# Loading and transposing the gate weights of a mixture-of-experts kernel: one word-wise DMA against GpSimd rows and six PE transposes

## The chip, the cores and the metric

The kernel runs on one core of one Trainium2 chip. The metric is device time in microseconds for one execution, input tensors in DRAM to output in DRAM. The profile names the engines PE (TensorE matmuls), PEld (its weight loads), DVE (VectorE), ACT (ScalarE), POOL (GpSimd) and SP (SyncE, which issues nearly all DMAs here).

## The reference, cut to what matters

Three stages follow one another: an attention with a sigmoid in place of the softmax, a layer that takes the maximum of three projections, and a mixture of 8 experts. The change touches one input of the third, the gate weights `w_gate` (768 x 8 float32, 24 KB), which choose one expert for each token.

```python
scores = scale * np.matmul(q, k.transpose(0, 1, 3, 2)) - np.log(S)      # 4 x 12 heads, S = 448, D = 64
x = 1 / (1 + np.exp(-scores)) @ v                                      # -> 1792 tokens x 768
h = np.maximum(np.maximum(x @ w1, x @ w2), x @ w3)
x = h @ w_out
logits = x @ w_gate + modality_bias[modality_id]                       # w_gate: 768 x 8
e_idx = np.argmax(logits, axis=1)                                      # one expert of 8 for each token
...
out[mask] = gate_w[mask, None] * (np.maximum(x[mask] @ w1[e], 0) @ w2[e])
```

## The kernel before

The attention stage works on 24 units of two heads each, in 12 pairs (the loop over `j`, L379). For a unit, `split_qk` (L267, on DVE) splits the loaded q and k into a rounded part and a rest in `kq`; `emit_qk` (L287, on PE) makes the scores in three groups of six matmuls, each group followed by a sigmoid on ACT (L285); `emit_av` (L315, on PE) multiplies with v; `emit_qk_last` (L303) and `emit_av_last` (L323) do the last 64 of the 448 columns for both units of a pair; `evac_X` (L331, on DVE) brings the result into SBUF. The order on PE, ACT, DVE and SP is the order in which the code is written, and each engine runs its instructions in that order; GpSimd's come in the order of the code too. SP runs two pairs ahead: in pair j, behind `emit_qk_last(j)`, it issues the loads of q, k and v for the units of pair j + 2 (L254 to L265), and from the second pair on, in most second pairs, one chunk of the projection weights of the second stage (`stage`, L216), which DVE converts from 64-bit words a little at a time (`background`, L236).

`wgT` is a DRAM scratch tensor that holds the gate weights turned, as 8 rows of 768. Its only readers are eight DMAs in the second stage (L436), each of which spreads one row over all partitions; DVE then folds the gate weights into `w_out` (L439). The first of these is issued at 236.6 us of the span. In the fifth pair (j = 4) SP issues, ahead of that pair's weight chunk, four small transfers: `slots` (L400), `wgT` (L402), the modality bias `mb` (L403) and the modality numbers `midi` (L404). The transfer at L402 reads `w_gate` word by word so that it lands turned; `midi` is read in words of 8 bytes, 1792 of them; `mb` is 128 copies of 64 bytes.

At the start PE runs seven matmuls on constants (`warm`, L356) while the first loads are on their way, and GpSimd fills constants, the identity matrix `ident` among them. The tile `v4` (tag K1) holds the v of two units of six; in the second stage the same space holds the gate rows. PSUM tags: the scores go round `a0`, `a1` and `t`; `x0` and `x1` hold the results of the units, and `x1` the warm-up before them.

Of the kernel before, what the change touches and what calls it, by code (L numbers as in the profile page):

```python
# [28 lines left out]
def attn_moe_kernel(  # L29
# [15 lines left out]
    nc = tc.nc  # L45
    B, HP, D, _, _, S = qk.shape
    NT, DM = out.shape
    E, _, FF = ew1.shape
    KB = DM // 128
# [25 lines left out]
    def hold(tag, name, *shape):  # L75
        return pool.tile([128, *shape], F32, tag=tag, name=name)

    def r(ap):
        return ap.bitcast(F32R)

    def cut(a, off, *shape):

        n = 1
        for s in shape:
            n *= s
        a = a[:, off:off + n]
        if len(shape) == 2:
            a = a.rearrange("p (a b) -> p a b", a=shape[0])
        elif len(shape) == 3:
            a = a.rearrange("p (a b c) -> p a b c", a=shape[0], b=shape[1])  # L90
        return a
# [10 lines left out]
    NW = 2 * NJ  # L102
# [5 lines left out]
    kq = [cut(kq_, 4 * S * i, 2, 2, S) for i in range(2)]  # L108
    u1, u2, u3 = (hold(f"U{i}", f"u{i}", 2048) for i in range(3))
    qk_in = [cut(u, 2 * S * i, 2, S) for u in (u1, u2) for i in range(2)]  # L110
    v4 = hold("K1", "v4", 2, NW + 1, D)
    v_in = [cut(u3, (NW + 1) * D * i, NW + 1, D) for i in range(4)] + [v4[:, i] for i in range(2)]

    stage = [hold(f"S{i}", f"stage{i}", KB * 256).bitcast(I32) for i in range(2)]
# [7 lines left out]
    wgT = dram.tile([E, DM], F32, name="wgT")  # L122
# [3 lines left out]
    ident = cpool.tile([128, 128], F32, name="ident")  # L126
# [21 lines left out]
    def ps(tag, shape, name):  # L148
        return psum.tile(shape, F32, tag=tag, name=name)
# [60 lines left out]
    def load_chunk():  # L210
        i = loaded[0]
        if i < len(chunks):
            kind, a, b = chunks[i]
            loaded[0] += 1
            src, n = chunk_src(a, b) if kind == "w" else (woi[a * 128:(a + 1) * 128, :].rearrange("p (a c) -> p a c", a=1), 1)
            nc.sync.dma_start(out=stage[i % 2].rearrange("p (a c) -> p a c", a=n), in_=src)  # L216
# [19 lines left out]
    def background(us, stop=None, late=2):  # L236

        while us > 0 and (bg or bg2):
            if stop is not None and stop in ready:
                return  # L240
            if bg and (bg[0][2] is None or step[0] >= used.get(bg[0][2], 1e9) + late):
                op, cost, _ = bg.popleft()
            elif bg2 and loaded[0] > LAST_O and step[0] >= bg2[0][2]:
                op, cost, _ = bg2.popleft()
            else:
                return
            op()
            us -= cost


    def load_qk(u):
        b, hp = divmod(u, HP)
        for h in range(2):
            nc.sync.dma_start(out=qk_in[u % 4][D * h:D * (h + 1)], in_=qk[b, hp, :, h])  # L254

    def load_v(u):
        b, hp = divmod(u, HP)
        vt = v_in[u % 6]
        if u % 2 == 0:
            nc.sync.dma_start(out=vt, in_=v[b, hp])  # L260
            return

        nc.sync.dma_start(out=vt[:, 0:NW], in_=v[b, hp, :, 0:NW])
        for h in range(2):
            nc.sync.dma_start(out=vt[SR * (1 - h):SR * (2 - h), NW], in_=v[b, hp, SR * h:SR * (h + 1), NW])  # L265

    def split_qk(u):  # L267
        src, kt = qk_in[u % 4], kq[u % 2]
        if u == 0:
            nc.vector.tensor_copy(out=r(kt[:, 0, 0]), in_=src[:, 0])  # L270
            nc.scalar.activation(out=r(kt[:, 0, 1]), in_=src[:, 1], func=ACTF.Copy)
            for i in range(2):
                nc.vector.tensor_tensor(out=r(kt[:, 1, i]), in0=src[:, i], in1=kt[:, 0, i], op=ALU.subtract)
        else:
            nc.vector.tensor_copy(out=r(kt[:, 0]), in_=src)  # L275
            nc.vector.tensor_tensor(out=r(kt[:, 1]), in0=src, in1=kt[:, 0], op=ALU.subtract)
# [3 lines left out]
    def scores():  # L280
        s_n[0] += 1
        return ps(("a0", "a1", "t")[s_n[0] % 3], [128, 2, 512], "s")

    def sigmoid(dst, s):
        nc.scalar.activation(out=dst, in_=s[:, :, 0:S], func=ACTF.Sigmoid, scale=qscale, bias=nlns)  # L285

    def emit_qk(u):  # L287

        kt = kq[u % 2]
        for g in range(NJ):  # L290
            s = scores()
            for n, (a, x) in enumerate(((0, 0), (0, 1), (1, 0))):
                for h in range(2):
                    p = slice(D * h, D * (h + 1))
                    nc.tensor.matmul(s[:, h, 0:S], r(kt[p, a, 0, 128 * g:128 * (g + 1)]), r(kt[p, x, 1]),  # L295
                                     start=(n == 0), stop=(n == 2))
            sigmoid(atb[u % 2][:, 2 * g:2 * g + 2], s)

    def quarter(i, h):

        return slice(SR * (h ^ i), SR * ((h ^ i) + 1))

    def emit_qk_last(j):  # L303

        s = scores()
        for i in range(2):
            src = qk_in[(2 * j + i) % 4]
            for h in range(2):
                p = slice(D * h, D * (h + 1))
                nc.tensor.matmul(s[quarter(i, h), i, 0:S], src[p, 0, 128 * NJ:], src[p, 1], start=True, stop=True)  # L310
        sigmoid(atl[j % 2], s)
# [3 lines left out]
    def emit_av(u):  # L315
        X_t[u] = ps(f"x{u % 2}", [128, 512], "X")
        vt, at = v_in[u % 6], atb[u % 2]
        for g in range(NJ):
            for h in range(2):
                nc.tensor.matmul(X_t[u][64 * h:64 * h + 64, 0:S], vt[:, 2 * g + h], at[:, 2 * g + h],  # L320
                                 start=(g == 0), stop=False)

    def emit_av_last(j):  # L323
        for i in range(2):
            u = 2 * j + i
            for h in range(2):
                p = quarter(i, h)
                nc.tensor.matmul(X_t[u][64 * h:64 * h + 64, 0:S], v_in[u % 6][p, NW], atl[j % 2][p, i],  # L328
                                 start=False, stop=True)

    def evac_X(u):  # L331
        b, hp = divmod(u, HP)
        src = X_t.pop(u)[:, 0:S]
        dR = xR[hp][:, b * S:(b + 1) * S]
        dL = xL[hp][:, b * S:(b + 1) * S]
        nc.vector.tensor_copy(out=r(dR), in_=src)
        nc.vector.tensor_tensor(out=r(dL), in0=src, in1=dR, op=ALU.subtract)

    with tc.manual_schedule(engines={mybir.EngineType.PE, mybir.EngineType.Activation, mybir.EngineType.DVE, SP}):
        load_qk(0)  # L340
        nc.vector.memset(gw, 0.0)
        nc.vector.memset(ones, 1.0)
        make_identity(nc, ident)
# [35 lines left out]
        for j in range(NU // 2 + 1):  # L379
            A, B, more = 2 * j, 2 * j + 1, j < NU // 2  # L380
            if more:
                emit_qk(A)
            if j:
                emit_av(B - 2)
                emit_av_last(j - 1)
                evac_X(A - 2)
                evac_X(B - 2)
            if not more:
                break
            emit_qk_last(j)  # L390
            for u in (A + 4, B + 4):
                if u < NU:
                    load_qk(u)
                    load_v(u)
            if A + 2 < NU:
                split_qk(A + 2)
            if j == 1:
                load_chunk()
            if j == 4:
                nc.sync.dma_start(out=slots.rearrange("(p c) o -> p (c o)", p=128), in_=idx)  # L400
                with nc.allow_non_contiguous_dma(reason="small"):
                    nc.sync.dma_start(out=wgT, in_=w_gate.rearrange("d e -> e d"))  # L402
                nc.sync.dma_start(out=mb, in_=m_bias.partition_broadcast(128))  # L403
                nc.sync.dma_start(out=midi, in_=mid.bitcast(I32).rearrange("(i p t) -> p i t", p=128, t=2))  # L404
            if j >= 2:
                background(2.5, stop=(1, 0))
            emit_qk(B)
            emit_av(A)
            if B + 2 < NU:
                split_qk(B + 2)  # L410
# [491 lines left out]
        for p, (i, n) in enumerate(todo[:NF * NCH]):  # L902
# [9 lines left out]
            else:  # L912
                f = n - 2 * KB
# [27 lines left out]
        d = xo[xo_n[0] % 3]  # L941
# [7 lines left out]
    with tc.For_i(NSTAT, nreg, 1) as iv:  # L949
        nc.sync.dma_start(out=idx2, in_=slots.rearrange("(p c) o -> p (c o)", p=128)[:, bass.ds(iv * 2, 2)])  # L950
        nc.sync.dma_start(out=e_dyn, in_=exd[0:1, bass.ds(iv, 1)])
        e = nc.values_load(e_dyn[0:1, 0:1], engines=(SP,), min_val=0, max_val=E - 1)
# [51 lines left out]
```

## Time and profile before

| what | us |
|---|---|
| median of 3 runs (807.14 to 807.71) | 807.19 |
| the profiled execution's own time | 807.75 |
| its span, first to last instruction | 806.0 |
| PE busy in the span | 760.3 (94%) |
| DVE, ACT, POOL busy | 448.5, 258.6, 65.2 |

The profile is of one execution, and all its times are microseconds from the start of its span unless they are marked ns; 1.75 us of the execution's time lie around the span. A row of an engine in order of time has the start, the length, the engine, the line of the kernel, the operation with what it writes and reads, and the count of instructions merged into the row; in brackets is the idle time of the engine ahead of it and what ended it. A row of SP's queue is the time in which SP was busy with issuing DMAs, not that of their transfer. The row of a stretch has the busy time and the count of instructions of each engine, the clock granted to PE (1.00 is 2.4 GHz, 0.50 is 1.2 GHz), the mean busy share of the 16 DMA engines, and the rate of the bytes moved.

### The profile page before, as it was taken

Reading aid. Unit: us, or ns where it says so; the run is one execution under the profiler, and the core shown is the slowest. Engines: PE = TensorE matmul, PEld = TensorE weight load, DVE = VectorE, ACT = ScalarE, POOL = GpSimd, SP = SyncE. Lnnn points to the kernel's source line nnn. Section 1 sums busy time; section 2 is a strip of 40 time slices with the busy share of each in tenths; the row PEclk is TensorE's granted clock in tenths of the full one; section 3 lists DMA queues with packets and bytes.
Section 4 is the critical chain, followed back from the end, with each engine's and each line's share of the span. In section 5 each row is a group of like instructions: output and inputs, shape, how many; then the busy total and the mean of one; then the engine's idle time right before and its main releaser. Section 6 shows DMA issues by size and latency. Waiting matters only on the chain.

```text
span 806.0 us, 11821 instructions
## 1 busy us (share of the span) xinstructions
PE 760.3 (94%) x4698; PEld 642.0 (80%) x4698; DVE 448.5 (56%) x751; ACT 258.6 (32%) x362; POOL 65.2 (8%) x82
## 2 busy tenths in 40 slices
PE   9998059999999999999999999999999999999994
PEld 5454034479999999999997888998999999899993
DVE  3685047666696878784305822246665466555532
ACT  5665025520101010010003323245544445454522
POOL 0000000000000000000010060230220302021000
PEclk9999569999999999999999999999999999999998
DMA  8767596313242131220000196343657401064000
GB/s 206 206 148 2 3 225 164 109 40 118 77 153 83 59 117 59 79 79 1 0 1 1 54 368 243 102 144 133 249 171 263 157 22 59 14 246 148 20 25 18
DMA packets 50920, 88.04 MB, mean 109 GB/s; under 512 B 14219, under 2 KB 32908, under 8 KB 50862
## 3 DMA queue, kind: packets, MB, share of 16 engines
q1 hardware_dynamic: 47294, 75.71, 33.1%
q0 software_dynamic: 3568, 11.54, 4.3%
q8 instruction: 39, 0.64, 0.3%
q14 instruction: 19, 0.16, 0.1%
HBM read 94.95 MB, written 11.57 MB: 132 GB/s over the span
## 4 chain that ended last, share of the span: by engine, by line
PE 87%; SPq 6%; issue 2%; DMA 2%; DVE 1%; POOL 0%; ACT 0%; POOLq 0%; DVEq 0%
PE acc L457 33%; PE oacc L796 15%; PE hacc L775 14%; PE acc L523 7%; PE X L320 6%; PE s L295 5%; SPq L403 4%; PE acc2b L523 4%; DMA u<-in_qk_dram 2%; PE X L328 1%; PE xT L736 1%; PE s L310 1%; SPq L254 1%; PE lgp L483 1%; SPq L216 1%
## 5 line engine op out<-in xcount | busy, mean ns | idle before, releaser
L457 PE MATMUL acc<-xR,w_ring 128*128 128x448 f32 x864 | 210.5, 365 | 0.0
L457 PEld LDWEIGHTS acc<-xR,w_ring 128*128 128x128 f32 x864 | 162.2, 188 | 13.5 <-issue 0.7
L796 PE MATMUL oacc<-wo_ck,xh 128*128 128x512 f32 (+1 forms) x672 | 124.0, 340 | 0.0
L775 PE MATMUL hacc<-xh,wo_ck 128*128 128x256 f32 x1008 | 122.3, 283 | 0.0
L775 PEld LDWEIGHTS hacc<-xh,wo_ck 128*128 128x128 f32 x1008 | 121.9, 192 | 0.3
L796 PEld LDWEIGHTS oacc<-wo_ck,xh 128*128 128x128 f32 x672 | 102.8, 188 | 13.8
L285 ACT ACTIVATE at<-s,nlns 128x896 f32<-128x896 f32 x84 | 78.2, 1008 | 80.8 <-PE s L295 51.3
L457 PE MATMUL acc<-xLa,w_ring 128*128 128x448 f32 x360 | 102.2, 365 | 0.0
L295 PE MATMUL s<-kq 64*128 64x448 f32 x432 | 53.7, 388 | 31.8 <-DVE kq L275 31.2
L295 PEld LDWEIGHTS s<-kq 64*128 64x128 f32 x432 | 38.8, 190 | 54.2 <-issue 39.7
L182 DVE TENSOR_TENSOR wo_ck<-raw,wo_ck 128x512 fp32r<-128x512 f32 (+1 forms) x108 | 75.4, 743 | 6.0 <-ACT wo_ck L181 5.8
L523 PE MATMUL acc<-wo_ck,hs 128*128 128x512 f32 x252 | 77.4, 394 | 0.0
L457 PEld LDWEIGHTS acc<-xLa,w_ring 128*128 128x128 f32 x360 | 67.6, 188 | 5.3
L181 ACT ACTIVATE wo_ck<-raw 128x512 fp32r<-128x512 f32 (+1 forms) x108 | 67.0, 671 | 11.5 <-PE hacc L775 11.3
L523 PEld LDWEIGHTS acc<-wo_ck,hs 128*128 128x128 f32 x252 | 47.2, 188 | 11.4 <-ACT wo_ck L181 0.8
L523 PE MATMUL acc2b<-wo_ck,hs 128*128 128x256 f32 x252 | 56.2, 280 | 0.0
L439 DVE SCALAR_TENSOR_TENSOR gk<-wof,gk 128x768 f32<-128x768 f32 x48 | 45.9, 956 | 1.2
L461 ACT ACTIVATE hA<-acc 128x896 f32<-128x896 f32 x8 | 7.4, 920 | 115.1 <-PE acc L457 115.1
L782 DVE SCALAR_TENSOR_TENSOR xh<-hacc,xh 128x1024 fp32r<-128x1024 f32 x14 | 17.1, 1224 | 46.3 <-ACT xh L781 46.3
L727 POOL DMA_INDIRECT xg<-x2d,idx x30 | 30.0, 1000 | 148.2 <-PE xT L736 101.0
L523 PEld LDWEIGHTS acc2b<-wo_ck,hs 128*128 128x128 f32 x252 | 41.5, 189 | 0.1
L320 PE MATMUL X<-at,u 128*64 128x448 f32 x192 | 40.4, 557 | 0.0
(175 smaller groups left out, 666.5 us busy)
## 6 DMA issues: line engine op xcount, KB each, us to landing
raw<-in_moe_w_dram SPq DMA_DIRECT2D x24, 1024.0 KB
stage<-in_moe_w_dram SPq DMA_DIRECT2D x18, 768.0 KB
u<-in_qk_dram SPq DMA_DIRECT2D x48, 224.0 KB
raw<-in_moe_w_dram SPq DMA_DIRECT2D x12, 768.0 KB
raw_S<-in_moe_w_dram SPq DMA_DIRECT2D x12, 768.0 KB
stage<-in_moe_w_out_dram SPq DMA_DIRECT2D x6, 768.0 KB
x2d<-xo SPq DMA_DIRECT2D x14, 256.0 KB
gk<-wgT SPq DMA_DIRECT2D x8, 384.0 KB
```

Of the source, the lines that this page charges most:

```text
L181: nc.scalar.activation(out=r(dR), in_=src, func=ACTF.Copy)
L182: nc.vector.tensor_tensor(out=r(dL), in0=src, in1=dR, op=ALU.subtract)
L285: nc.scalar.activation(out=dst, in_=s[:, :, 0:S], func=ACTF.Sigmoid, scale=qscale, bias=nlns)
L295: nc.tensor.matmul(s[:, h, 0:S], r(kt[p, a, 0, 128 * g:128 * (g + 1)]), r(kt[p, x, 1]), start=(n == 0), stop=(n == 2))
L320: nc.tensor.matmul(X_t[u][64 * h:64 * h + 64, 0:S], vt[:, 2 * g + h], at[:, 2 * g + h], start=(g == 0), stop=False)
L403: nc.sync.dma_start(out=mb, in_=m_bias.partition_broadcast(128))
L439: nc.vector.scalar_tensor_tensor(out=junk, in0=wof[kb], scalar=1.0, in1=wgb[e % 2], op0=ALU.mult, op1=ALU.mult, accum_out=gw[:, kb, e:e + 1])
L457: nc.tensor.matmul(acc[:, c, 0:S], r(m[:, a, kk, :]), r(x[kk][:, c0 + S * c:c0 + S * (c + 1)]), start=(kk == 0 and n == 0), stop=(kk == KB ...
L523: nc.tensor.matmul(acc_t[t, c], r(hs[t][:, a, kk, :]), r(wo_rl[c][:, kk, b]), start=(kk == 0 and n == 0), stop=(kk == KB - 1 and n == 2))
L727: nc.gpsimd.indirect_dma_start(out=xg[i % 2][s][:, XC[c][0]:XC[c][1]], out_offset=None, in_=x2d[c], in_offset=bass.IndirectOffsetOnAxis(ap ...
L775: nc.tensor.matmul(acc[:, f], r(w[a][:, 128 * f:128 * (f + 1)]), r(x[:, kk]), start=(kk == 0 and m == 0 and f % 2 == 0), stop=(kk == KB - ...
L796: nc.tensor.matmul(dst, r(x[:, f, 128 * s:128 * (s + 1)]), r(w[a][:, c0:c1]), start=(f == 0 and m == 0 and not (shared and s == 1)), stop= ...
```

## The change

The word-wise DMA at L402 goes. In its place:

- GpSimd's queue, as its first instruction behind the program's start, loads `w_gate` in rows of 8 words (32 bytes; 128 partitions times 6 rows, 768 in all) into `wg_in`, a piece of the K1 tile that now is one tile of 2304 words a partition.
- In the first pair, behind `emit_qk_last(0)`, `turn_gate` puts six PE transposes (8 columns by 128 rows each) into PSUM tags `x0` and `x1`, and two DVE copies (8 x 512 and 8 x 256) into `wg_t`.
- GpSimd's queue writes `wg_t` to `wgT`, 8 rows of 3072 bytes, behind the constants.

```diff
--- before.py
+++ after.py
@@ -108,7 +108,10 @@
     kq = [cut(kq_, 4 * S * i, 2, 2, S) for i in range(2)]
     u1, u2, u3 = (hold(f"U{i}", f"u{i}", 2048) for i in range(3))
     qk_in = [cut(u, 2 * S * i, 2, S) for u in (u1, u2) for i in range(2)]
-    v4 = hold("K1", "v4", 2, NW + 1, D)
+    k1 = hold("K1", "k1", 3 * DM)
+    v4 = cut(k1, 0, 2, NW + 1, D)
+    wg_in = cut(k1, 2 * (NW + 1) * D, KB, E)
+    wg_t = k1[0:E, 2 * DM:3 * DM]
     v_in = [cut(u3, (NW + 1) * D * i, NW + 1, D) for i in range(4)] + [v4[:, i] for i in range(2)]
 
     stage = [hold(f"S{i}", f"stage{i}", KB * 256).bitcast(I32) for i in range(2)]
@@ -328,6 +331,15 @@
                 nc.tensor.matmul(X_t[u][64 * h:64 * h + 64, 0:S], v_in[u % 6][p, NW], atl[j % 2][p, i],
                                  start=False, stop=True)
 
+    def turn_gate():
+
+        for x, k0, k1 in ((0, 0, 4), (1, 4, KB)):
+            T = ps(f"x{x}", [128, 512], "wgp")
+            for k in range(k0, k1):
+                nc.tensor.transpose(T[0:E, 128 * (k - k0):128 * (k - k0 + 1)], wg_in[:, k], ident)
+            nc.vector.tensor_copy(out=wg_t[:, 128 * k0:128 * k1], in_=T[0:E, 0:128 * (k1 - k0)])
+        nc.gpsimd.dma_start(out=wgT, in_=wg_t)
+
     def evac_X(u):
         b, hp = divmod(u, HP)
         src = X_t.pop(u)[:, 0:S]
@@ -338,6 +350,7 @@
 
     with tc.manual_schedule(engines={mybir.EngineType.PE, mybir.EngineType.Activation, mybir.EngineType.DVE, SP}):
         load_qk(0)
+        nc.gpsimd.dma_start(out=wg_in, in_=w_gate.rearrange("(k p) e -> p k e", p=128))
         nc.vector.memset(gw, 0.0)
         nc.vector.memset(ones, 1.0)
         make_identity(nc, ident)
@@ -388,6 +401,8 @@
             if not more:
                 break
             emit_qk_last(j)
+            if not j:
+                turn_gate()
             for u in (A + 4, B + 4):
                 if u < NU:
                     load_qk(u)
@@ -398,8 +413,6 @@
                 load_chunk()
             if j == 4:
                 nc.sync.dma_start(out=slots.rearrange("(p c) o -> p (c o)", p=128), in_=idx)
-                with nc.allow_non_contiguous_dma(reason="small"):
-                    nc.sync.dma_start(out=wgT, in_=w_gate.rearrange("d e -> e d"))
                 nc.sync.dma_start(out=mb, in_=m_bias.partition_broadcast(128))
                 nc.sync.dma_start(out=midi, in_=mid.bitcast(I32).rearrange("(i p t) -> p i t", p=128, t=2))
             if j >= 2:
```

Lines of the kernel after are higher by 3 from L112 to L330, by 12 to L340, by 13 to L390, by 15 to L400 and by 13 from L403 on (numbers of the kernel before). In the rows below, `u` and `v` or `k` with a number are SBUF buffers, and the brackets name the semaphores waited for: DMASW that of a DMA from GpSimd's queue, DMAHW those of SP's, in turn eight of each, so that each DMA also waits for the one eight before it.

SP's queue, in the pair j = 4, before:

```order
L265 DMA u_73<-in_v_dram 64x64 [waits DMAHW1_49]
L400 DMA slots<-idx 128x30 [waits DMAHW2_49,Pool_49]
L402 DMA wgT<-in_moe_w_gate_dram 6144x1x1 [waits DMAHW3_49]
L403 DMA mb<-in_moe_modality_bias_dram 128x16 [waits DMAHW4_49]
L404 DMA midi<-in_moe_modality_id_dram 128x14x2 [waits DMAHW5_49]
L216 DMA stage_75<-in_moe_w_dram 128x6x256 [waits DMAHW6_49]
L254 DMA u_72<-in_qk_dram 64x896 [waits DMAHW7_49,DVE_49,PE_49]
```

and after:

```order
L268 DMA u_73<-in_v_dram 64x64 [waits DMAHW1_49]
L415 DMA slots<-idx 128x30 [waits DMAHW2_49,Pool_49]
L416 DMA mb<-in_moe_modality_bias_dram 128x16 [waits DMAHW3_49]
L417 DMA midi<-in_moe_modality_id_dram 128x14x2 [waits DMAHW4_49]
L219 DMA stage_75<-in_moe_w_dram 128x6x256 [waits DMAHW5_49]
L257 DMA u_72<-in_qk_dram 64x896 [waits DMAHW6_49,DVE_49,PE_49]
```

The four small transfers have become three; `mb`, `midi`, the chunk of weights and the next pair's loads follow `slots` in the same order, and each waits for the semaphore one number lower.

PE, in the first pair, before:

```order
L310 MATMUL s<-u_71 64x448 [waits DMAHW3_49]
L295 MATMUL s<-kq 128x448 [waits DVE_49,Activation_49]
L295 MATMUL s<-kq 128x448
L295 MATMUL s<-kq 128x448 [waits DVE_49]
L295 MATMUL s<-kq 128x448 x3
L295 MATMUL s<-kq 128x448 [waits Activation_49]
```

and after:

```order
L313 MATMUL s<-u_71 64x448 [waits DMAHW3_49]
L339 MATMUL wgp<-ident,k_74 8x128 [waits DMASW0_49,Pool_49]
L339 MATMUL wgp<-ident,k_74 8x128 x5
L298 MATMUL s<-kq 128x448 [waits DVE_49,Activation_49]
L298 MATMUL s<-kq 128x448
L298 MATMUL s<-kq 128x448 [waits DVE_49]
L298 MATMUL s<-kq 128x448 x3
L298 MATMUL s<-kq 128x448 [waits Activation_49]
```

The six transposes stand between `emit_qk_last(0)` and the scores of unit 1; the first waits for the rows of GpSimd's DMA and for the identity matrix.

DVE, in the first pair, before:

```order
L275 CAST kq<-u_71 128x896 [waits DMAHW3_49,DMAHW2_49]
L276 TENSOR_TENSOR kq<-u_71,kq 128x896 [waits DVE_49]
L275 CAST kq<-u_72 128x896 [waits DMAHW1_49,DMAHW0_49,PE_49]
L276 TENSOR_TENSOR kq<-u_72,kq 128x896 [waits DVE_49]
L275 CAST kq<-u_72 128x896 [waits DMAHW3_49,DMAHW2_49,PE_49]
```

and after:

```order
L278 CAST kq<-u_71 128x896 [waits DMAHW3_49,DMAHW2_49]
L279 TENSOR_TENSOR kq<-u_71,kq 128x896 [waits DVE_49]
L340 COPY k_74<-wgp 8x512 [waits PE_49]
L340 COPY k_74<-wgp 8x256 [waits PE_49]
L278 CAST kq<-u_72 128x896 [waits DMAHW1_49,DMAHW0_49]
L279 TENSOR_TENSOR kq<-u_72,kq 128x896 [waits DVE_49]
```

Two copies that wait for PE stand ahead of the split of unit 2.

## Rows read from the trace of the kernel before

**Rows 1.** The page's 40 slices of 20.15 us: PE's busy share in tenths

```profile
PE   9998059999999999999999999999999999999994
```

**Rows 2.** PE in order, 71.9 to 125: start us, us, instructions, idle before, releaser

```profile
72.72 0.93 PE L310 MATMUL s<-u 64*64 64x448 f32 x8
...
75.67 2.48 PE L320 MATMUL X<-at,u 128*64 128x448 f32 x12
109.37 0.74 PE L295 MATMUL s<-kq 64*128 64x448 f32 x2 [31.22 <-DVE kq L275]
...
117.73 0.93 PE L310 MATMUL s<-u 64*64 64x448 f32 x8
```

**Rows 3.** PE in order, 159 to 161: the last pair's rows of L310

```profile
160.04 0.93 PE L310 MATMUL s<-u 64*64 64x448 f32 x8
```

**Rows 4.** DVE in order, 74 to 110

```profile
74.78 0.62 DVE L337 TENSOR_TENSOR xLb<-X,xR 128x448 fp32r<-128x448 f32 x1
108.59 0.63 DVE L275 CAST kq<-u 128x896 fp32r<-128x896 f32 x1 [33.19 <-DMA u<-in_qk_dram]
```

**Rows 5.** SP's queue in order, 57 to 110: issues of DMAs

```profile
58.09 0.81 SPq L402 DMA_DIRECT2D wgT<-in_moe_w_gate_dram  x1
58.95 30.48 SPq L403 DMA_DIRECT2D mb<-n_moe_modality_bias_dram  x1
89.47 0.43 SPq L404 DMA_DIRECT2D midi<-in_moe_modality_id_dram  x1
89.95 4.43 SPq L216 DMA_DIRECT2D stage<-in_moe_w_dram  x1
```

**Rows 6.** Packets that the DMA engines moved from 61 to 90 us

```profile
DMA packets 5572, 0.04 MB, mean 1 GB/s; under 512 B 5571, under 2 KB 5571, under 8 KB 5571
```

**Rows 7.** Packets that the DMA engines moved from 91 to 99 us

```profile
DMA packets 1494, 0.02 MB, mean 3 GB/s; under 512 B 1491, under 2 KB 1494, under 8 KB 1494
```

**Rows 8.** Stretches: length, busy of five engines, granted clock, DMA share, GB/s

```profile
61.00:91.00 30.00, 17.14 (x126) 8.02 (x122) 11.01 (x16) 10.21 (x11) 0.00 (x0) 0.84 0.80 1
91.00:96.00 5.00, 0.00 (x0) 0.00 (x0) 0.00 (x0) 0.00 (x0) 0.00 (x0) 0.50 0.03 1
96.00:98.50 2.50, 0.00 (x0) 0.00 (x0) 0.00 (x0) 0.00 (x0) 0.00 (x0) 0.50 0.55 7
```

**Rows 9.** PE in order, 5.6 to 20.8: the first pair

```profile
6.12 0.49 PE L295 MATMUL s<-kq 64*128 64x448 f32 x2
...
9.63 2.63 PE L295 MATMUL s<-kq 64*128 64x448 f32 x18
12.20 2.48 PE L320 MATMUL X<-at,u 128*64 128x448 f32 x12
14.61 2.09 PE L295 MATMUL s<-kq 64*128 64x448 f32 x18
...
19.83 0.93 PE L310 MATMUL s<-u 64*64 64x448 f32 x8
```

**Rows 10.** DVE in order, 0 to 13

```profile
5.26 0.39 DVE L270 CAST kq<-u 128x448 fp32r<-128x448 f32 x1 [3.96 <-DMA u<-in_qk_dram]
...
10.64 0.63 DVE L275 CAST kq<-u 128x896 fp32r<-128x896 f32 x1 [1.68 <-PE s L295]
11.30 1.09 DVE L276 TENSOR_TENSOR kq<-u,kq 128x896 fp32r<-128x896 f32 x1
```

**Rows 11.** The stretch in which the first loads arrive

```profile
2.00:5.00 3.00, 3.00 (x11) 3.00 (x10) 0.00 (x0) 0.30 (x2) 0.62 (x10) 1.00 0.95 233
```

**Rows 12.** PE in order, 523.9 to 525.4: transposes of other data

```profile
524.44 1.04 PE L736 MATMUL xT<-ident,xg 128*128 128x128 f32 x8
```

**Rows 13.** DVE in order, 439.9 to 441: a copy out of PSUM

```profile
440.37 0.41 DVE L511 COPY gk<-lgp 96x256 f32<-96x256 f32 x1
```

**Rows 14.** POOL in order, 518 to 524: DMAs that GpSimd issues

```profile
522.70 0.94 POOL L727 DMA_INDIRECT xg<-x2d,idx  x1 [0.30 <-issue]
```

**Rows 15.** POOL in order, 0.4 to 12: the identity matrix

```profile
1.21 0.28 POOL masks.py:199 TENSOR_SCALAR_AFFINE_SELECT ident<-ident 128x128 f32<-128x128 f32 x1
```

## The prediction

> **What bounds the kernel now.** The slices of the page come first [rows 1]: PE is busy nine tenths or more nearly everywhere, so time lost or won elsewhere counts only where PE waits for it. One place stands out: a hole in the fifth and sixth slices (81 to 121 us), in which the clock granted to PE falls to 0.50 [rows 8]. PE's own rows then give the hole's size [rows 2]: its work ends at 78.15 (75.67 + 2.48) and begins again at 109.37, 31.22 us later, released by DVE, which makes the next unit's `kq`. DVE in turn stood still for 33.19 us until a load of q and k landed at 108.59 [rows 4]. Why that load was late stands in SP's queue [rows 5]: it issued the word-wise DMA of L402 at 58.09 in 0.81 us, and the next one, L403, kept it for 30.48 us. All else that SP had to issue was queued behind that, first the loads of units 14 and 15. What the DMA engines did meanwhile is in their packets [rows 6]: 5571 packets below 512 bytes between 61 and 90 us, at a mean busy share of 0.80 and about 1 GB/s [rows 8]. Only L402's 6144 words can be so many: `mb` has 128 pieces, and `midi` was not issued before 89.47 [rows 5]. So the chain is: words of L402 fill the queue, SP is held, loads are late, DVE waits, PE waits.
>
> What the hole costs is read from the rhythm of the pairs, not from the idle time alone, since PE starts again at half its clock. L310 runs once for each pair. From 19.83 to 72.72 are five pairs [rows 2, 9], from 117.73 to 160.04 four [rows 2, 3]; both give 10.58 us a pair. Between 72.72 and 117.73 lie 45.01 us. The excess is **34.43 us**: 31.22 idle, and 3.21 in which PE runs slowly behind the hole.
>
> **The change, part by part.**
>
> *L402 goes.* SP can then issue `mb`, `midi`, the weight chunk and the next loads as soon as their buffers are free. PE is the bound before and after the hole at the same 10.58 us a pair, and DVE, ACT and SP stand still in the hole along with it, so no work was done there that has to be made up later. What comes out is the whole excess: -34.43. What is late next is `midi` (first rival).
>
> *768 rows of 32 bytes on GpSimd's queue, at the start.* They share the DMA engines with the loads of units 0 and 1, at a share of 0.95 from 2 to 5 us [rows 11]. Unit 0 has no cover: DVE takes it at 5.26 [rows 10], and PE begins the scores at 6.12 [rows 9], just where its warm-up ends, so a delay there passes to the end in full. The price of a small packet has two rows. `midi` and `mb` go from DRAM to SBUF, as `wg_in` does: 1491 packets [rows 7], nearly all of them in 2.5 us at a share of 0.55 [rows 8], are 1.38 us of all engines, so 768 are 1.38 x 768 / 1491 = 0.71 us. L402's words, from DRAM to DRAM, took 30 x 0.80 = 24 us for 5571 [rows 6, 8], so 768 would be 3.3 us. Nothing is lost if GpSimd has issued them only when unit 0 is in; the later loads have slack. A gain is excluded, since nothing at the start is taken away. I take the price of `midi`, the like transfer, and half of it, as whether the words come ahead of unit 0's last packets is open: +0.35 (0 to 0.71; 3.3 is a rival).
>
> The Trainium skill ("DMA: Bandwidth & Descriptors", "Rules for kernel authors") says that DMAs issued from several engines run on the same 16 DMA engines and interleave, so that spreading them brings no bandwidth. By that the whole 0.71 would stand in the sum and the result would be 0.36 us later; no row of the kernel before shows two queues at that time.
>
> *The wait of PE for these rows.* Nearest are the DMAs that GpSimd issues later: 0.94 us for one of 128 rows, at 522.70 [rows 14], and PE has the data 1.74 us after its start, at 524.44 [rows 12]. GpSimd is at the program's own instructions by 1.2 [rows 15]. If the issue grows with the rows, 6 x 0.94 = 5.6, they land at 1.2 + 5.6 + 0.8 = 7.6; if not, at 2.9. PE comes to its transposes at 9.63 [rows 9], so it waits for neither: 0. The identity matrix, ready at 1.49 now (1.21 + 0.28), is queued behind on GpSimd and comes 5.6 us later at worst, at 7.1. The other constants are first read hundreds of us later.
>
> *Six transposes on PE.* Eight others take 1.04 us [rows 12], 0.13 each, so six are 0.78. Behind them are the scores of unit 1. These take 2.63 us there against 2.09 in the next unit [rows 9], as they wait for the sigmoids in between; this 0.54 is cover. What is left is +0.24 (0 to 0.78).
>
> *Two copies on DVE.* A copy of 256 elements out of PSUM takes 0.41 [rows 13]; 512 and 256 are at most 0.82 + 0.41 = 1.23. They wait for PE until about 9.63 + 0.78 = 10.4 and end by 11.7. The split of unit 2 queued behind them starts at 10.64 now [rows 10], so it is 1.1 us late; it ends at 12.39 now (11.30 + 1.09) and PE needs it at 14.61 [rows 9], 2.2 us later. PSUM `x0` is free again by about 11.2, before the products of unit 0 at 12.20 [rows 9]. Cost 0; without that cover it would be 1.1.
>
> *The write of `wgT`.* Eight rows of 3072 bytes, some 200 us ahead of the first reader, and GpSimd has nothing else to do: 0.
>
> *Sum.* 806.0 - 34.43 + 0.35 + 0.24 = 772.16 us of span. The profiled execution had 1.75 us around its span and stood 0.56 above the median: 772.16 + 1.75 - 0.56 = 773.35, so **773.4 us**.
>
> **The rivals.**
>
> *`midi` takes L402's place.* Its 1792 words of 8 bytes stay in SP's queue ahead of the chunk and the loads. For it: from its issue at 89.47 [rows 5] to the landing of the load at 108.59 [rows 4] passed 19.1 us, the chunk kept SP for 4.43 us behind it [rows 5], and from 91 to 96 the engines stood nearly idle [rows 8]. Against it: part of this may be the end of L402's own words. If all of it comes again, moved from the end of L402's flow (91) to the time when the loads of the fifth pair are through (61, since from there on 1 GB/s flows [rows 8]), the load lands at 78.6. PE works until 78.15 [rows 2] and starts 0.78 after DVE (109.37 - 108.59 [rows 2, 4]); it would idle for 78.6 + 0.78 - 78.15 = 1.2 us. It decides from a landing at 77.4 on. Time: 774.6.
>
> *The words at the start cost what L402's cost.* 3.3 us in place of 0.35, all of it ahead of unit 0: 776.3. For it: L402 is the only large flow of single words in the trace. Against it: L402 wrote 4-byte words into DRAM, and `midi` into SBUF is at a fifth of that.
>
> *Slower: the 768 rows go one after another.* If GpSimd's DMA puts them all through one DMA engine at L402's price, 24 x 16 / 5571 = 69 ns each, they land at about 1.2 + 53 = 54, PE waits from 9.63 on for 44.4 us and starts at half its clock (3.2 as above): 773.4 + 44.4 + 3.2 = 821.0. It decides from a wait of about 31 us on, a landing after 41. Against it: a DMA of 128 rows from GpSimd's queue is with PE after 1.74 us [rows 12, 14], where 128 x 69 ns would be 8.8.
>
> *The change doesn't do what it says:* the hole is `mb`'s and `midi`'s, and stays: 807.19 + 0.59 = 807.8. Against it are the 5571 packets [rows 6].
>
> **How the numbers follow.** The forecast has 0.70, `midi` 0.13, dear words 0.13, one by one 0.02, no effect 0.02. A measurement of this kernel tells about 0.2%, 1.6 us, from no change; so faster has 0.96, same 0.02, slower 0.02. The forecast's own bounds are 0.59 below (no cost at all, 772.8) and 0.90 above (0.71 + 0.78 - 0.59, 774.3). With the spread of the runs (0.6 us) the low end is 772.3; the high end takes in `midi` at the upper bounds (775.5) and the cheaper part of the dear words, 776.0. Left out are most of the dear words and the last two, under 0.2 together.
>
> **What would show it.** Right: L310's rows keep 10.58 us through the seventh pair, SP's issue of `mb` lasts below 1 us, PE's clock stays at 1.00 there, and packets below 512 bytes fall by some 5400. First rival: DVE idles at about 75.4 for a load and PE at about 78. Dear words: PE's first scores come at 8 to 9 instead of 6.12. Late rows: PE idles ahead of L339, released by a DMA of `wg_in`. The forecast would be wrong if a wait in a later stage took the 34 us back; PE is the bound there too, with the same order of work, so I see none.

## The result, and the profile after

The changed kernel takes **776.09 us** (median of 4 executions, 774.83 to 776.54); the kernel before, run beside it, 807.16 us (4 executions, 806.36 to 807.71). The ratio is 0.9613, with a 95% interval of 0.9597 to 0.9630. That is 31.1 us less, where 33.8 were forecast; the median lies 2.7 us above the forecast and 0.09 above the range's upper end, which the four executions straddle. The profiled execution is the shortest of them: 774.83 us, of which 773.0 are its span.

The page's slices, 19.3 us each, answer [rows 1]: PE's busy share in tenths, and the clock granted to it.

```profile
PE   8999999999999999999999999999999999999993
...
PEclk9999999999999999999999999999999999999997
...
DMA packets 44833, 88.07 MB, mean 114 GB/s; under 512 B 8107, under 2 KB 26812, under 8 KB 44774
```

The hole in the fifth and sixth slices is gone, and PE is busy for 98% of the span. SP's queue shows why; these rows (start, length, what was issued) answer [rows 5]:

```profile
59.22 0.57 SPq L415 DMA_DIRECT2D slots<-idx  x1
59.83 0.43 SPq L416 DMA_DIRECT2D mb<-n_moe_modality_bias_dram  x1
60.31 0.43 SPq L417 DMA_DIRECT2D midi<-in_moe_modality_id_dram  x1
60.78 0.79 SPq L219 DMA_DIRECT2D stage<-in_moe_w_dram  x1
63.88 1.11 SPq L257 DMA_DIRECT2D u<-in_qk_dram  x2
```

`mb` keeps SP for 0.43 us instead of 30.48, and the weight chunk behind `midi` for 0.79 instead of 4.43. The loads of the next units follow at 63.88. On PE, the rows of L313 (L310 before), one for each pair, stand 10.58 us apart right through the place where 45.01 us lay [rows 2]:

```profile
62.94 0.93 PE L313 MATMUL s<-u 64*64 64x448 f32 x8
73.52 0.93 PE L313 MATMUL s<-u 64*64 64x448 f32 x8
84.09 0.93 PE L313 MATMUL s<-u 64*64 64x448 f32 x8
94.68 0.93 PE L313 MATMUL s<-u 64*64 64x448 f32 x8
```

No row of PE between 60 and 130 us has any idle time ahead of it. In the stretch that had a clock of 0.84 and 1 GB/s [rows 8], the clock is now 1.00 and 185 GB/s flow (columns: length, busy time and count of PE, PEld, DVE, ACT, POOL, clock, DMA share, GB/s):

```profile
61.00:91.00 30.00, 30.00 (x222) 14.85 (x220) 23.38 (x35) 17.78 (x20) 0.00 (x0) 1.00 0.79 185
```

The words of L402 are gone from the packets too. The page of the kernel before has this line, to be set beside the last one of the first block above:

```profile
DMA packets 50920, 88.04 MB, mean 109 GB/s; under 512 B 14219, under 2 KB 32908, under 8 KB 50862
```

Packets below 512 bytes fell from 14219 to 8107, by 6112, and not by the 5400 that were forecast: the forecast took the 768 rows for 768 packets. How they came is in GpSimd's row, and in two lines on the first 10 us: its queue (number 0) with packets, MB and share of 16 engines, and the transfer with its size and the us from issue to landing.

```profile
1.38 1.02 POOL L353 DMA_DIRECT2D k<-in_moe_w_gate_dram  x1 [0.85 <-POOLq L1002]
...
q0 software_dynamic: 32, 0.02, 2.2%
...
k<-in_moe_w_gate_dram POOLq DMA_DIRECT2D x1, 24.0 KB, 4.5
```

They went as 32 packets, which took 2.2% of 10 us, 0.22 us of all engines, and landed 4.5 us after the start of their issue, at 5.9.

The price is at the start. DVE's first row and PE's rows of the first pair answer [rows 9, 10]:

```profile
5.86 0.39 DVE L273 CAST kq<-u 128x448 fp32r<-128x448 f32 x1 [4.57 <-DMA u<-in_qk_dram]
...
9.32 0.98 PE L313 MATMUL s<-u 64*64 64x448 f32 x8
10.23 0.82 PE L339 MATMUL wgp<-ident,k 128*8 128x128 f32 x6
10.98 2.09 PE L298 MATMUL s<-kq 64*128 64x448 f32 x18
13.01 2.48 PE L323 MATMUL X<-at,u 128*64 128x448 f32 x12
...
20.64 0.93 PE L313 MATMUL s<-u 64*64 64x448 f32 x8
```

Unit 0 reaches DVE at 5.86 instead of 5.26 us, and the second pair's L313 stands at 20.64 instead of 19.83: 0.81 us later, of which 0.60 are the load of unit 0 and 0.21 the transposes. The span is then accounted for: the pairs give 34.43 us, the start takes 0.81, and 0.6 are lost behind the last matmul, where the last scatter of the output starts 10.8 us before the span's end instead of 10.2 (762.18 of 773.0, 795.79 of 806.0). 806.0 - 34.43 + 0.81 + 0.61 = 773.0.

### The profile page after: what moved, and what is told of

Read it like the earlier page. It is cut to its first block, busy times and chain, and to the rows that moved or that the text cites. A ratio compares the mean times of both kernels' runs of the same rounds, so it can differ in the third digit from the quotient of the medians.

```text
span 773.0 us, 11840 instructions
## 1 busy us (share of the span) xinstructions
PE 758.0 (98%) x4704; PEld 641.3 (83%) x4704; DVE 449.4 (58%) x753; ACT 258.3 (33%) x362; POOL 67.4 (9%) x84
## 2 busy tenths in 40 slices
DMA packets 44833, 88.07 MB, mean 114 GB/s; under 512 B 8107, under 2 KB 26812, under 8 KB 44774
## 4 chain that ended last, share of the span: by engine, by line
PE 94%; issue 2%; DMA 1%; DVE 0%; POOL 0%; ACT 0%; SPq 0%; POOLq 0%; DVEq 0%
PE acc L470 34%; PE oacc L809 15%; PE hacc L788 15%; PE acc L536 8%; PE X L323 7%; PE s L298 6%; PE acc2b L536 4%; PE X L331 1%; PE s L313 1%; PE xT L749 1%; PE lgp L496 1%; DMA u<-in_qk_dram 1%; DMA x2d<-xo 0%; PE hacc L941 0%; DMA xg<-x2d,idx 0%
## 5 line engine op out<-in xcount | busy, mean ns | idle before, releaser
L298 PE MATMUL s<-kq 64*128 64x448 f32 x432 | 51.3, 378 | 0.6 <-DVE kq L276 0.3
```

## The experiments

Each of these kernels was compared with the kernel before on its own chip, and each ratio is against that. They ran on three other chips, on which the kernel before took 810.65 to 814.09 us.

**The change again, and where its start costs.** The first kernel is the changed one, on a second chip.

> The changed kernel once more, as the measure for the other three of this batch. Theory A (what comes out is the 34.4 us excess of the seventh pair, and what goes in stands wholly in the first 20 us: unit 0 lands 0.6 us late behind the 768 rows, the transposes add 0.2 us): about 772.8 + 0.8 = 773.6 to 775. Theory B (the GpSimd rows cost some 2 us more in executions other than the profiled one, which was 1.3 us under the median): 776 again, and a trace that shows unit 0 landing later than 5.86 us or PE at half its clock near the start.

It took 778.14 us (777.57 to 778.71; before 810.65), ratio 0.9588 (0.9561 to 0.9616). Unit 0 came at 5.50 us and the second pair at 20.33. So the gain repeats, with the start a little cheaper. Carried over to the first chip by its ratio, it would be 773.9 us (0.9588 x 807.16), which is in theory A's range; the interval, 771.7 to 776.2, doesn't exclude theory B's time, but the two signs that B named for the trace are absent. What is new stands in the second projection, which took 92.8 us here and 89.5 in the trace of the first chip; more on that below.

The next one lets SP issue the same rows, behind the loads of unit 1's q and k; the transposes stay.

```diff
-        nc.gpsimd.dma_start(out=wg_in, in_=w_gate.rearrange("(k p) e -> p k e", p=128))
         ...
         load_qk(1)
+        nc.sync.dma_start(out=wg_in, in_=w_gate.rearrange("(k p) e -> p k e", p=128))
```

> The changed kernel with one edit: the 768 rows are issued by SP behind the loads of units 0 and 1, not by GpSimd at the start; the transposes stay. Theory A: unit 0 lands at 5.26 us again, the transposes cost 0.2 us: 0.6 us under the changed kernel. Theory B: 2 to 3 us under it, within 0.5 us of the kernel with the late words. Rival: SP's issues shift by 0.5 us and the rows land after 9.6 us, so that PE waits ahead of the transposes: up to 1.5 us over theory A.

It took 778.56 us (776.74 to 778.98), ratio 0.9589 (0.9560 to 0.9618). DVE and PE in order, at the start:

```profile
5.25 0.39 DVE L273 CAST kq<-u 128x448 fp32r<-128x448 f32 x1 [3.95 <-DMA u<-in_qk_dram]
...
8.73 0.98 PE L313 MATMUL s<-u 64*64 64x448 f32 x8
9.65 0.82 PE L339 MATMUL wgp<-ident,k 128*8 128x128 f32 x6
```

Unit 0 is back at 5.25 us, as in the kernel before, and the second pair at 20.08: what is left of the delay, 0.2 us, is the transposes'. So the rows delay unit 0 where GpSimd issues them at the start; whether the queue or the place matters isn't separated, as the edit changes both. On SP's queue the same rows are 768 packets (8875 below 512 bytes on that run's page, 8107 in the changed kernel). In the time, the few tenths can't be seen.

**The words without the queue behind them.** If the words of L402 cost only what is queued behind them, they may stay single words and go elsewhere. First behind the last loads of the stage, at j = 10, with no rows and no transposes:

```diff
             if j == 4:
                 nc.sync.dma_start(out=slots.rearrange("(p c) o -> p (c o)", p=128), in_=idx)
-                with nc.allow_non_contiguous_dma(reason="small"):
-                    nc.sync.dma_start(out=wgT, in_=w_gate.rearrange("d e -> e d"))
...
+            if j == 10:
+                with nc.allow_non_contiguous_dma(reason="small"):
+                    nc.sync.dma_start(out=wgT, in_=w_gate.rearrange("d e -> e d"))
```

> The kernel before with one edit: the word-wise DMA moves from the pair j = 4 to the pair j = 10, behind the last loads of q, k and v; no rows, no transposes. Theory A: the hole of 34.4 us is gone and nothing is added: 772.7 (807.16 - 34.4), unit 0 at 5.26 us, the pairs 10.58 us apart throughout. SP is held some 30 us, but only ahead of weight chunks that wait for DVE anyway. Theory B: the same 772.7, at least 3 us under the changed kernel. Theory C (any kernel without the hole loses some 2 us elsewhere, at its end): about 775.3. Rival: the words hold up the weight chunks of the second stage and PE waits there, above 780.

It took 778.01 us (777.36 to 786.78), ratio 0.9612 (0.9559 to 0.9665). SP's queue and PE in order:

```profile
111.80 30.10 SPq L216 DMA_DIRECT2D stage<-in_moe_w_out_dram  x1
...
158.80 0.67 PE L458 MATMUL acc<-xR,w_ring 128*128 128x448 f32 x2 [2.55 <-DVE hA L464]
```

SP is held for about as long as before, but the pairs run through (the last instruction of L310 starts at 126.0 us), and unit 0 comes at 5.17. In the changed kernel the issue of the same chunk keeps SP for half a microsecond:

```profile
111.01 0.53 SPq L219 DMA_DIRECT2D stage<-in_moe_w_out_dram  x1
```

So the words themselves cost next to nothing; what costs is what stands behind them in SP's queue. Here two weight chunks stand there, and PE pays 2.6 us in the first projections.

The same with the rows loaded at the start by GpSimd as well, and never read, should add the start's cost alone:

```diff
+        nc.gpsimd.dma_start(out=wg_in, in_=w_gate.rearrange("(k p) e -> p k e", p=128))
```

> As the kernel with the late words, and GpSimd loads the 768 rows at its start as in the changed kernel, though nothing reads them: the start's price alone, without transposes. Theory A: 0.6 us over the kernel with the late words, unit 0 at 5.86 us. Theory B: 2 to 3 us over it. Theory C: 0.6 over it, both near 775 to 776.

It took 782.47 us (779.85 to 787.13), ratio 0.9648 (0.9607 to 0.9689). Unit 0 came at 5.68 us, 0.51 later than without the rows, which is the start's cost once more. The total says little of it: PE waited 2.4 us in the projections as in the run ahead, but then fell to half its clock for a moment, and for the rest of that stage it ran 2% slower at full clock (921 matmuls from 200 to 390 us, where the changed kernel has 940). The stage took 271.6 us instead of 262.6. The profile names no cause for the 2%; no other run has it.

At the end of j = 9, ahead of that pass's background work, the words might be through before the chunk is needed:

```diff
+            if j == 9:
+                with nc.allow_non_contiguous_dma(reason="small"):
+                    nc.sync.dma_start(out=wgT, in_=w_gate.rearrange("d e -> e d"))
```

> The kernel before with the word-wise DMA moved from pair j = 4 to the end of pair j = 9, just behind the last loads of q, k and v; one pair earlier than in the late words, where the chunk queued behind it kept DVE for 12 us and PE for 2.4. Theory A: the chunk lands some 10 us earlier, about when DVE wants it, so PE waits nowhere: first pair as in before, 0.6 to 0.8 us under the changed kernel. Rival: PE still waits 1 to 2 us in the projections.

It took 782.37 us (777.2 to 787.23), ratio 0.9621 (0.9546 to 0.9695). SP's queue, DVE and PE in order:

```profile
111.27 0.81 SPq L405 DMA_DIRECT2D wgT<-in_moe_w_gate_dram  x1
112.19 28.56 SPq L216 DMA_DIRECT2D stage<-in_moe_w_out_dram  x1
...
157.96 0.56 DVE L165 TENSOR_SCALAR cv<-stage 128x768 int32<-128x768 int32 x1 [14.09 <-DMA stage<-in_moe_w_out_dram]
...
160.76 1.00 PE L458 MATMUL acc<-xR,w_ring 128*128 128x448 f32 x2 [4.33 <-DVE hA L464]
```

The hoped-for gain isn't there: the words reach SP's queue at 111.27 us, not sooner, and the chunk behind them lands so late that DVE waits 14.09 us and PE 4.33. For SP the edit changes nothing: in the run with the words at j = 10, too, they come right behind the last loads, at 110.89 us, and ahead of the two chunks. The two medians, 778.01 and 782.37, stand in ranges that overlap (777.36 to 786.78 and 777.2 to 787.23).

Cut into eight transfers of 768 words, one in each of the passes 2 to 9, no one of them should hold SP for long:

```diff
+            if 2 <= j < 2 + E:
+                with nc.allow_non_contiguous_dma(reason="small"):
+                    nc.sync.dma_start(out=wgT[j - 2:j - 1], in_=w_gate[:, j - 2:j - 1].rearrange("d e -> e d"))
```

> The kernel before with the same 6144 words in eight DMAs of 768, one at the end of each pair from j = 2 to 9. Theory A (the words cost 5 ns each of SP's queue, and each pair's loads have some 12 us of slack, so that only a large burst is seen): each holds SP for some 4 us, nothing waits, pairs stay 10.58 us apart; 0.6 to 0.8 us under the changed kernel, like the words at j = 9. Rival (any word-wise DMA stalls the loads behind it): each pair grows by 1 us or more, 8 us over the changed kernel or worse.

It took 790.22 us (789.28 to 793.68), ratio 0.9747 (0.9707 to 0.9786), worse than any place but the first. The pairs end 11.2 us later than in the run with the words at j = 10 (the last instruction of L310 starts at 137.2 against 126.0). SP, DVE and PE in order at the worst of them:

```profile
75.77 5.59 SPq L265 DMA_DIRECT2D u<-in_v_dram  x2
...
82.66 0.63 DVE L275 CAST kq<-u 128x896 fp32r<-128x896 f32 x1 [7.32 <-DMA u<-in_qk_dram]
...
83.44 0.74 PE L295 MATMUL s<-kq 64*128 64x448 f32 x2 [5.36 <-DVE kq L275]
```

That is far less than the hole of before, since no load is held for 30 us. The 11.2 us aren't eight equal delays: 8.6 of them lie between the pairs' rows at 72.65 and 91.83, 19.18 us apart instead of 10.58, where the load of a unit was late once more; the other 2.6 come in the last pairs. SP's row of 5.59 us holds two short issues. Ahead of each SP waited for the transfer eight before it (what waited and for what; us, times, longest):

```profile
SPq L265 <- DMA stage<-in_moe_w_dram: 4.6, 1, 4.6
SPq L265 <- DMA wgT<-in_moe_w_gate_dram: 4.5, 1, 4.5
```

One of the two was a part of the words, the other the weight chunk issued right behind it. So theory A fails. The rival holds in its total, 8 us over the changed kernel or worse (790.22 against 778.55 on this chip), and not in its form, as most pairs did not grow by 1 us. In three stretches with one of the eight under way, the DMA engines are at a share of 0.72 to 0.79 and move 29 to 96 GB/s for 6 to 10 us; if the others are like these (an estimate), all eight take longer than the one of 6144 words with its 30.48.

**What a single word costs.** Same words, same place (j = 4), but written into SBUF (8 partitions of 768); GpSimd then writes the block to `wgT`.

```diff
-                    nc.sync.dma_start(out=wgT, in_=w_gate.rearrange("d e -> e d"))
+                    nc.sync.dma_start(out=wg_t, in_=w_gate.rearrange("d e -> e d"))
+                nc.gpsimd.dma_start(out=wgT, in_=wg_t)
```

> The kernel before with one edit at L402: the same 6144 words, in the same place of SP's queue, but written into SBUF (8 partitions x 768) in place of DRAM; GpSimd's queue then writes 8 rows to wgT. No rows at the start, no transposes. Theory A1 (what is dear in L402 is the single-word write into DRAM; words into SBUF cost what those of midi cost, 0.9 ns each of all engines): 6144 x 0.92 = 5.7 us of SP's queue, the next loads land before DVE wants them, no hole, pairs 10.58 us apart, about 0.8 us under the changed kernel. Theory A2 (any 6144 words cost what L402 cost, by the count of words): the hole stays as in the kernel before, about 32 to 34 us over the changed kernel.

It took 784.65 us (781.92 to 788.12; on a third chip, before 813.85), ratio 0.9626 (0.9594 to 0.9659). SP's queue:

```profile
58.27 0.84 SPq L404 DMA_DIRECT2D k<-in_moe_w_gate_dram  x1
59.16 12.23 SPq L406 DMA_DIRECT2D mb<-n_moe_modality_bias_dram  x1
71.44 0.43 SPq L407 DMA_DIRECT2D midi<-in_moe_modality_id_dram  x1
71.92 1.89 SPq L218 DMA_DIRECT2D stage<-in_moe_w_dram  x1
```

12.23 us lie between the two ends that were expected, the price of `midi`'s words and that of L402's. So the number of words alone doesn't set how long the queue is held: 12.23 / 6144 = 2.0 ns a word into SBUF, 30.48 / 6144 = 5.0 ns into DRAM. Whether the destination makes the difference, or the form that changed with it (8 partitions of 768 words instead of a list of 6144), isn't separated. Even so the loads come late: the last instruction of L310 starts at 134.3 us, with one wait of PE of 5.6.

At j = 9, where 28.56 us were too long, 12 should do. This joins the two edits above.

> The single words of the gate weights go into SBUF instead of DRAM, and are issued at the end of the pass j = 9 of the first stage, ahead of that pass's background work; GpSimd then writes the turned block into wgT. No rows at the start, no transposes. Theory: the queue is held for about 12 us, as in the run that wrote them into SBUF in their first place (12.23), and the chunk queued behind it lands before VectorE asks for it at about 140 us. Then unit 0's first product stands at 5.2 to 5.3 us, the second pair at 19.8 to 19.9, all pairs 10.58 us apart, the projection stage takes 262.6 us as in the changed kernel, and the ratio to the kernel before is 0.956 to 0.961. Rival: the chunk is still late for its conversion; PE waits 1 to 4 us for VectorE in the first projections, and the ratio is 0.961 to 0.966.

It took 780.04 us (779.19 to 780.39; on a fourth chip, before 814.09), ratio 0.9580 (0.9561 to 0.9600). SP's queue:

```profile
110.11 1.59 SPq L407 DMA_DIRECT2D k<-in_moe_w_gate_dram  x1
111.81 9.46 SPq L218 DMA_DIRECT2D stage<-in_moe_w_out_dram  x1
```

SP is held for 9.46 us, less than the 12 of the theory; no wait of PE in the first projections is left, they take 262.6 us, and the second pair stands at 19.79. For the rest the theory holds. The projections begin at 134.1 us, 0.8 ahead of the changed kernel on the first chip (134.9), with no wait in them to pay for it. In time it isn't told apart from the changed kernel, whose ratios of 0.9588 to 0.9613 have intervals that overlap with its own.

**The gap in the second projection.** On the second chip the kernel before was profiled again (one execution), and the changed kernel once more beside it.

> The kernel before, for its trace on the same chip as the others of this batch. The traces of the last batch all had a gap of some 3 us in the second projection (PE with L536 or L523 at 2.00 us busy of 2.00 before, at 0.3 to 1.7 in three windows near 447 us, ended by nothing the profile shows), which the first traces of before and after don't have. Theory A (that gap belongs to the chip and the execution, not to the change): before has it or lacks it along with the others here. Theory D (the change brings it, by moving that stage 34 us earlier): before never has it, and the changed kernel has it here.

> The changed kernel on this chip. Theory A: in the trace the pairs 10.58 us apart, unit 0 at 5.4 to 5.9 us in place of 5.2 to 5.3, the transposes 0.2 us net; the end of PE's work 33.6 us earlier than in the trace of before, but for the gap in the second projection where one of the two has it.

The kernel before took 811.48 us, with unit 0 at 5.33 and the second pair at 19.90; the hole was 29.7 us of idle PE and an excess of 32.8 (43.39 - 10.58) rather than 34.43. The changed kernel took 778.55 us (777.74 to 780.35), ratio 0.9596 (0.9564 to 0.9629), with unit 0 at 6.03. In both traces PE, which was gapless in the second projection on the first chip, stumbles there. Stretches of the kernel before, on the second chip:

```profile
475.00:480.00 5.00, 3.98 (x23) 3.35 (x22) 0.45 (x1) 0.00 (x0) 3.78 (x5) 1.00 1.01 389
480.00:485.00 5.00, 3.44 (x11) 2.51 (x11) 1.57 (x5) 2.29 (x5) 0.38 (x1) 0.74 0.28 101
```

The changed kernel on the third chip shows it larger:

> The changed kernel, as the measure for the two others of this batch: if the gap of the second projection is on this chip too, some 3 us more than 89.5 us from the first to the last of L536.

It took 781.10 us (780.34 to 781.36), ratio 0.9591 (0.9565 to 0.9616). Its stretches:

```profile
440.00:445.00 5.00, 5.00 (x31) 4.39 (x30) 0.69 (x1) 0.63 (x1) 3.78 (x5) 1.00 1.03 394
445.00:450.00 5.00, 2.44 (x8) 1.34 (x8) 0.00 (x0) 0.00 (x0) 2.67 (x3) 0.92 0.53 203
450.00:455.00 5.00, 4.58 (x15) 3.90 (x16) 2.33 (x7) 2.43 (x5) 0.00 (x0) 0.50 0.47 137
```

PE, DVE and ACT all but stop together, PE's matmuls waiting for nothing that the profile shows, and then PE runs at half its clock; the second projection takes 96.4 us instead of 89.5. In each of these traces GpSimd is at the end of its 14 scatters of `slots`, single words into DRAM, which run from 430.39 to 448.28 us here. To see whether the gap belongs to them, they were moved by three passes:

```diff
-            if t == 2:
+            if t == 5:
                 route_slots(pr)
```

> The changed kernel with one edit: the routing step that ends in 14 scatters of 128 single words each into the DRAM tensor slots comes behind token tile 5 in place of 2, some 18 us later. Theory E (the gap of the second projection, in which all engines stand with nothing that the profile shows, is the end of these single-word writes into DRAM, like the 5 us in which nothing moved behind L402's words): the gap moves with them, from 48 us behind the first L496 to 60 or later. Theory F (the gap belongs to the place in the program or to the expert weight loads there): it stays at 48 us.

It took 779.44 us (776.09 to 783.13), ratio 0.9586 (0.9537 to 0.9635). The last scatter starts at 465.92 us, and the gap has moved with it:

```profile
445.00:450.00 5.00, 5.00 (x30) 4.34 (x30) 4.00 (x21) 1.54 (x3) 1.06 (x1) 1.00 1.04 410
...
460.00:465.00 5.00, 4.70 (x22) 3.59 (x20) 0.46 (x1) 0.42 (x1) 3.78 (x5) 1.00 0.04 9
465.00:470.00 5.00, 3.14 (x14) 2.56 (x15) 1.85 (x5) 2.15 (x5) 1.58 (x2) 1.00 0.23 81
```

The expert weight loads that theory F names are not needed for it: just ahead of PE's idle time the DMA engines now move 9 GB/s, and 394 in the run above. So the gap follows the routing step that ends in the scatters, and since it is there before and after, it isn't the change's. Its size may differ between executions: this kernel's four took 776.09, 776.66, 782.23 and 783.13 us, and the profiled one is the second of these. On the first chip the same scatters ended without it. Why they end in it elsewhere is open.

## Why the prediction was right, and where it was off

- **The mechanism** held, link by link. Without L402's words SP issued `mb` in 0.43 us, the loads came in time, DVE and PE did not wait, and the pairs kept 10.58 us. The whole excess of 34.43 us came out, the 3.21 of the slow restart with it. That the words cost through what is queued behind them, and not by themselves, is shown by the run with the words at j = 10: SP is held there for 30.10 us, and PE waits 2.6.
- **The rows at the start** were put at +0.35 (0 to 0.71); the profiled execution has +0.60. Six traces with rows on GpSimd's queue have unit 0 at 5.50 to 6.03 us (mean 5.72), eight without at 5.17 to 5.33 (mean 5.25): 0.47. The bounds held, but the working behind them did not: it priced 768 packets like those of `midi`, and 32 were moved, which took 0.22 us of all engines. That two thirds of `midi`'s price came out is therefore luck. How 32 packets put off unit 0 by more than their own time is open. By the rule of the Trainium skill that the prediction weighed ("DMA: Bandwidth & Descriptors", "Rules for kernel authors"), DMAs of several engines interleave on the same 16 DMA engines. The trace agrees: from 3.5 to 5 us GpSimd's queue moved its 32 packets while SP's moved 89.
- **The wait of PE for the rows** was put at 0, and there was none: PE came at 10.23. GpSimd's issue of 768 rows took 1.02 us, so it did not grow with the rows. They landed at 5.9 all the same, between the two cases named (2.9 and 7.6), as the landing came 4.5 us after the start of the issue and not 1.74. PE had 4 us to spare. The identity matrix was ready at 3.1.
- **The six transposes** were put at +0.24. From unit 0's conversion to the second pair pass 14.78 to 14.84 us in six traces with them (mean 14.82), 14.55 to 14.75 in eight without (mean 14.59): 0.23. The cover that the prediction named was there: the scores behind them took 2.09 us instead of 2.63.
- **The two copies** took 1.01 us in all and put off the split behind them to 11.81; nobody waited for it.
- **The rivals.** `midi` did not take L402's place: DVE waits for no load at 75, and the chunk behind `midi` was issued in 0.79 us. So the 4.43 us, and the 19.1 from `midi`'s issue to the load, go with L402's words. The dear words fell with unit 0 at 5.86, and the serial rows and the change without effect with the traces as a whole.
- **The size** was 2.7 us short, in three pieces. The start took 0.22 more (0.81 against 0.59). The end of the span took 0.61 more, a tail that the sum had kept as it was. The rest, 1.9, is the step from the profiled execution to the median: the sum carried over 1.75 us around the span and a median 0.56 *below* the profiled execution, while here they were 1.83 and a median 1.26 *above* it. That term was mis-sized, and in the wrong direction: it was taken from one profile beside three executions. It has no fixed sign either: where the changed kernel ran again, the median stood 0.57 and 0.81 us above the profiled execution and 0.26 below it. What the other three executions did can't be seen, as they have no trace. That the gap in the second projection came up in them is possible, not shown: their mean granted clock was 0.992 to 0.994 against 0.995, but this kernel's traces with the gap have 0.990 to 0.996, so the clock doesn't tell. (The low end of the range comes to 772.2, not 772.3: 772.8 - 0.6. Nothing hangs on it.)

## What to carry to other kernels

A transfer of single words is paid for by whatever stands behind it in the same queue: look at the row *behind* it in the queue's own view, and at who has a date for what that row loads. Where it can't be avoided, put it behind the last load with a date, in one piece, and let it write into SBUF; parts strewn among the loads cost more than one piece behind them. A sum made against one profiled execution should carry the spread between executions in its range, also upward.

## What was not expected of the hardware

- A single word into DRAM held SP's queue for 4.6 to 5.0 ns (28.56 to 30.48 us for 6144 words), one into SBUF for 1.5 to 2.0 (12.23 us at j = 4, 9.46 at j = 9). The Trainium skill ("DMA: Bandwidth & Descriptors", "Rules for kernel authors") says that a strided last dimension becomes one descriptor per element; the 5571 packets [rows 6] agree, but by that alone both would cost the same. Why they differ is open.
- Behind the words into DRAM came, in the kernel before, 5 us in which the DMA engines stood nearly idle, at a share of 0.03 [rows 8], and again on the second chip, at 0.02. Behind those into SBUF in the same place there was none, nor behind those into DRAM at j = 10, so the destination alone doesn't bring it. Stretches behind the words, of the kernel before on the second chip, of the words into SBUF, and of the words at j = 10:

```profile
90.50:95.50 5.00, 0.00 (x0) 0.00 (x0) 0.00 (x0) 0.00 (x0) 0.00 (x0) 0.50 0.02 1
...
71.00:76.00 5.00, 5.00 (x42) 2.39 (x40) 2.66 (x5) 2.48 (x4) 0.00 (x0) 1.00 0.94 42
...
144.00:150.00 6.00, 6.00 (x31) 5.56 (x30) 0.00 (x0) 0.00 (x0) 0.00 (x0) 1.00 1.06 39
```

- Eight transfers of 768 words into DRAM, among the loads, cost the pairs 11.2 us, against 34.43 for one of 6144; one of 6144 into SBUF at that place cost less than either, 8.3 (134.3 instead of 126.0). Each is read from one profiled execution, and that of the words into SBUF is the slowest of its four (788.12 us).
- The scatters of single words to DRAM ended, on the chips beside the first one, in a stretch in which PE, DVE and ACT nearly stopped; in the longest of those shown the second projection took 6.9 us more (96.4 against 89.5), a part of it idle time of PE and a part at half its clock.
